# A linear-attention and ELU feed-forward kernel: the second tile cut to two blocks, W_out loaded earlier, and two blocks of second-layer work kept as filler

## The chip, the cores and the metric

The kernel runs on one core of a Trainium2 chip. The metric is the device time of one execution in microseconds (us), the median of several runs. One execution is also taken by the hardware profiler; its trace gives the start and end of every instruction.

The engines have short names in the profile: PE is TensorE's matmuls (PEld its weight loads), DVE is VectorE, ACT is ScalarE, POOL is GpSimd, SP is the engine that issues DMAs for outputs and transposes. A name with a q (SPq, POOLq) is that engine's instruction queue.

## The reference

Decayed linear attention over q, k, v of shape 4 x 8 x 768 x 64 (batch, heads, tokens, head size), then a two-layer feed-forward network with ELU on the 3072 tokens. All inputs and the output are float32.

```python
# attention, per batch and head, blocks of 64 tokens
intra = ((qb @ kb.T) * Dmask) @ vb          # Dmask[i, j] = lam ** (i - j) for i >= j, else 0
inter = (qb * lam_pow) @ kv_state           # lam_pow[i] = lam ** (i + 1)
out[block] = intra + inter
kv_state = lam ** 64 * kv_state + (kb * rev_pow).T @ vb

# feed-forward
x = out.transpose(0, 2, 1, 3).reshape(3072, 512)
h = x @ w_in                                # 512 -> 2048
g = where(h > 0, h, exp(min(h, 0)) - 1)
y = g @ w_out                               # 2048 -> 512
```

## The kernel before

**Blocks.** The kernel takes 128 tokens at a time. A block g (0 to 23) is one such chunk of one batch: g = 4 * chunk + batch, six chunks of four batches. In the change's title and in the prediction "chunk" is used for such a block: blocks 4 and 5 are the second chunk of tokens of batches 0 and 1. From g = 4 on the attention works on pairs (g, g + 1).

**Tiles.** The feed-forward network works on tiles of blocks. `TS` (L37) lists their sizes; `T0` gives each tile's first block and `where` maps a block to its tile and place. Before, there are six tiles of four blocks, 512 tokens each. The first layer of tile t has 16 slices of 128 of the 2048 hidden columns. Slice n takes four matmuls of up to 512 columns into a PSUM bank (`mm1_mm`, L424), then an exp and a relu on ScalarE (L450, L454) and one product on VectorE (L467) that gives g. Its buffers e and r have three copies each, so ScalarE can be at most three slices ahead of VectorE. For slices 2, 4 and 6 of tile 0 VectorE does the relu's part too (L462, L465). `mm1` has a branch for tiles of 256 tokens (`MT == 256`) that no tile takes before: it puts slices n and n + 1 side by side in one bank, and does exp, relu and product on both at once.

**Second layer.** `mm2(t, i, n)` (L499) adds the part of slice n to block i of tile t; after n = 15 the block is copied out of PSUM, by ScalarE for even i (L515) and VectorE for odd i (L513), and stored by SP (L516). The very last block is done by `mm2_last` (L479) in three pieces of 256, 128 and 128 columns.

**Attention of a pair g**, called a visit (`visit`): transposes of q and k on TensorE (`att_T`, L218) with copies by ScalarE (`att_Te`, L230), or for later pairs a DMA transpose on SP (`att_xT`, L274); scaled keys kd on VectorE (`att_kd`, L286); scores (`att_S`, L299); the decay mask on VectorE (`att_mask`, L311); outputs (`att_O`, L325 and L333); the state's update (`att_U`, L371); the outputs scaled into xt, the input of the first layer (`att_X`, L354); the new state on VectorE (`att_st`, L407); and the product of the old state with the decay for the next chunk on POOL (`att_tmp`, L388).

**Order.** Each engine executes in the order in which the program emits instructions. That order is written out by hand. `steps` is a list of (name, first-layer slice, second-layer parts). Steps ('A', 0..15) carry tile 0's first layer; ('B', 0..15) carry second-layer work alone; (1, 0) to (5, 15) carry tiles 1 to 5; ('E', 0) is the rest of the second layer. In each step the first layer's matmuls, exp and relu come first, then what was registered for the step with `at` (visits, loads, transposes), then the ELU product, then the second-layer matmuls:

```python
for s, m1, m2 in steps:
    ...
    er = mm1(t, n, alt=t == 0 and n in (2, 4, 6))
    do(s)
    if er:
        elu(t, n, *er)
    for t2, i2, n2 in m2:
        mm2(t2, i2, n2, "H" if t2 == 0 and m1 is None and i2 > 1 else "M")
```

**Loads.** All inputs are loaded and cast to float16 by DMAs that POOL issues, in the order of `LOADS`. An entry (g, 2) is three DMAs, q, k and v of a pair (L72); ('wi', i) is a piece of W_in (L97); ('wo', i) a quarter of W_out, four slices (L104); ('kd', g) is a product on POOL. The list is cut into stretches that are emitted at given steps, so POOL's products `tmp` stand between them. `XT` says at which step the DMA transposes of a pair are emitted on SP; SP also issues the stores, and waits for each in order.

**Before, around the change.** The second layer of blocks 0 and 1 begins at step ('A', 10); 36 more of its 64 matmuls with those of block 2 fill the B steps, beside the visits of pairs 4 and 6, on which tile 1 depends. Block 3 gives one matmul to each step of tile 1. From tile 2 on each step has four of the tile before. W_out's first two quarters are emitted before the steps, the third and fourth at ('A', 9) and ('A', 10), after the loads of pair 6.

Of the kernel before, what the change touches and what calls it, by code (L numbers as in the profile page):

```python
# [15 lines left out]
def kernel(  # L16
# [10 lines left out]
    nc = tc.nc  # L27

    B, H, S, D = q.shape
# [7 lines left out]
    TS = [4, 4, 4, 4, 4, 4]  # L37
    T0 = [sum(TS[:t]) for t in range(len(TS))]
    NT = len(TS)
    where = {T0[t] + i: (t, i) for t in range(NT) for i in range(TS[t])}  # L40

# [16 lines left out]
    kn = [cpool.tile([128, 2 * H, 64], FP16, name=f"kn_{i}") for i in range(NB)]  # L58
    vn = [cpool.tile([128, 2 * H, 64], FP16, name=f"vn_{i}") for i in range(NB)]

    def emit_load(g, n=1, which="qkv"):
        c, b = divmod(g, B)
        rows = slice(c * L, (c + 1) * L)
        i, o = (g // 2) % NB, (g % 2) * H
        for w, src in (("q", q), ("k", k), ("v", v)):
            if w not in which:
                continue
            if w == "v":
                dst = vn[i][:, o : o + n * H, :]
            else:  # L70
                dst = (qn if w == "q" else kn)[i][:, o : o + n * H, :]
            nc.gpsimd.dma_start(  # L72
                out=dst, in_=src[b : b + n, :, rows].rearrange("b h p d -> p (b h) d")
            )

    def heads(ts, g, n=1):
        o = (g % 2) * H
        return ts[(g // 2) % NB][:, o : o + n * H, :]
# [16 lines left out]
    def emit_wi(i):  # L95
        f0 = sum(WI[:i]) * 128
        nc.gpsimd.dma_start(  # L97
            out=wi_t[i][:],
            in_=moe_w_in[:, f0 : f0 + WI[i] * 128].rearrange("(k p) f -> p k f", p=128),
        )  # L100

    def emit_wo(i):
        f0 = sum(WO[:i]) * 128
        nc.gpsimd.dma_start(  # L104
            out=wo_t[i][:],
            in_=moe_w_out[f0 : f0 + WO[i] * 128, :].rearrange("(n p) f -> p n f", p=128),
        )
# [5 lines left out]
    LOADS = [(0, 1, 'q'), (0, 1, 'k'), (0, 1, 'v'), (1, 1, 'q'), (1, 1, 'k'), (1, 1, 'v'), (2, 1, 'q'), (2, 1, 'k'), (3, 1, 'q'), (3, 1, 'k'), (2, 1, 'v'), (3, 1, 'v'), ('wi', 0), ('wi', 1), ('wi', 2), ('wi', 3), ('wi', 4), ('wi', 5), ('kd', 0), ('wi', 6), ('kd', 2), ('wo', 0), (4, 2), ('wo', 1), (6, 2), ('wo', 2), ('wo', 3), (8, 2), (10, 2), (12, 2), (14, 2), (16, 2), (18, 2), (20, 2), (22, 2)]  # L113

    def run_loads(items):
        for it in items:
            if it[0] == "wi":
                emit_wi(it[1])
            elif it[0] == "wo":
                emit_wo(it[1])  # L120
            elif it[0] == "kd":
                att_kd(it[1], 2, "p")
            else:
                emit_load(*it)
# [53 lines left out]
    ks = cpool.tile([128, H], FP32, name="ks")  # L178
# [101 lines left out]
    def att_kd(g, n, eng="v"):  # L280
        if g // B == NC - 1:
            return
        kd = asb.tile([128, n * H, 64], FP16, tag="kd", name=f"kd{g}", bufs=2)
        ks_b = ks[:].unsqueeze(1).unsqueeze(3).broadcast_to([128, n, H, 64])
        e = nc.vector if eng == "v" else nc.gpsimd
        e.tensor_tensor(  # L286
            out=kd[:].rearrange("p (n h) d -> p n h d", n=n),
            in0=heads(kn, g, n).rearrange("p (n h) d -> p n h d", n=n),
            in1=ks_b, op=ALU.mult,
        )  # L290
        for i in range(n):
            kds[g + i] = kd[:, i * H : (i + 1) * H, :]
# [48 lines left out]
    def att_X(g, n, parts=1):  # L341
        t, i = where[g]
        if i == 0:
            xt[t] = asb.tile([128, HP, TS[t] * L], FP16, tag="xt", name=f"xt{t}")
        po = pS.pop(("O", g))
# [69 lines left out]
    def mm1_mm(t, n, lo, hi, tag="H"):  # L415

        if n == 0 and lo == 0:
            gt[t] = msb.tile([128, NF, TS[t] * L], FP16, tag="g", bufs=2, name=f"g{t}")
        if lo == 0:
            pH_of[t, n] = ps.tile([128, TS[t] * L], FP32, tag=tag, bufs=2, name=f"psH{t}_{n}")  # L420
        pH = pH_of[t, n]
# [49 lines left out]
    def mm2_last(t, i):  # L471

        c, b = divmod(T0[t] + i, B)
        t0 = b * S + c * L
        x0 = 0
        for x, (w, tag) in enumerate([(256, 'M'), (128, 'M'), (128, 'H')]):
            pm = ps.tile([128, w], FP32, tag=tag, bufs=2, name=f"psM{t}_{i}_{x}")
            for n in range(NF):
                nc.tensor.matmul(  # L479
                    pm[:], lhsT=gt[t][:, n, i * L : (i + 1) * L],  # L480
                    rhs=wo_t[wo_at[n][0]][:, wo_at[n][1], x0 : x0 + w],
                    start=(n == 0), stop=(n == NF - 1),
                )
            o = msb.tile([128, w], FP32, tag="osb", bufs=3, name=f"osl{x}")
            (nc.scalar.copy if x % 2 else nc.vector.tensor_copy)(o[:], pm[:])
            (nc.scalar if x % 2 else nc.sync).dma_start(
                out=out[t0 : t0 + L, x0 : x0 + w], in_=o[:]
            )
            x0 += w

    def mm2(t, i, n, tag="M"):
        if T0[t] + i == NG - 1:
            if n == NF - 1:
                mm2_last(t, i)
            return
        if n == 0:
            psM[t, i] = ps.tile([128, DM], FP32, tag=tag, bufs=2, name=f"psM{t}_{i}")
        pm = psM[t, i]
        nc.tensor.matmul(  # L499
            pm[:], lhsT=gt[t][:, n, i * L : (i + 1) * L],  # L500
            rhs=wo_t[wo_at[n][0]][:, wo_at[n][1], :], start=(n == 0), stop=(n == NF - 1),
        )
        if n < NF - 1:
            return
        c, b = divmod(T0[t] + i, B)
        t0 = b * S + c * L
        o = msb.tile([128, DM], FP32, tag="osb", bufs=3, name=f"osb{t}_{i}")
        last = T0[t] + i == NG - 1
        if last:
            raise AssertionError  # L510
        else:
            if i % 2:
                nc.vector.tensor_copy(o[:], pm[:])  # L513
            else:
                nc.scalar.copy(o[:], pm[:])  # L515
            nc.sync.dma_start(out=out[t0 : t0 + L, :], in_=o[:])  # L516
        psM.pop((t, i))
# [16 lines left out]
    def at(s, f, *a, **k):  # L534
        run.setdefault(s, []).append(lambda: f(*a, **k))
# [63 lines left out]

    run_loads(LOADS[17:25])  # L600
    for s, g in zip([], (0, 2)):
        at(s, att_kd, g, 2)
# [6 lines left out]
    XT = {10: (1, 2), 12: (1, 10), 14: (2, 2), 16: (2, 10), 18: (3, 2), 20: (3, 10), 22: (4, 2)}  # L609

    def visit(g, s0, s1, s2):
        if g in XT:
            at(XT[g], att_xT, g)
        else:
            at(s0, att_T, g, 2, "q")
            at(s0, att_T, g, 2, "k")
            at(s0, att_Te, g, 2, "q", "a")
            at(s0, att_Te, g, 2, "k", "v" if g in () else "a")
        if g not in ():
            at(s0, att_kd, g, 2, "p" if g in () else "v")  # L620
        at(s1, att_S, g)
        at(s1, att_S, g + 1)
        at(s1, att_mask, g)
        at(s1, att_mask, g + 1)
        if g in ():
            at(s1, att_kd, g, 2, "p" if g in () else "v")
        at(s2, att_O, g, 2)
        at(s2, att_U, g)
        at(s2, att_X, g, 2)
        at(s2, att_st, g)  # L630
        at(s2, att_tmp, g + B)

# [47 lines left out]
```

## Time and profile before

| | us |
|---|---|
| median of 5 runs (216.96 to 217.62) | 217.19 |
| the profiled execution's own time | 217.09 |
| its span, first to last instruction | 215.3 |
| TensorE busy (95% of the span) | 204.2 |
| VectorE busy (70%) | 151.4 |
| ScalarE busy (59%) | 127.5 |
| POOL busy (37%) | 80.1 |

The page gives busy time per engine, and the span in 40 slices of 5.4 us, each with a digit for the busy share in tenths. PEclk is the granted TensorE clock in the same tenths; the mean was 0.998. A matmul's length in the trace includes the tail of its pipeline, so the next one starts before it ends: the time that TensorE needs is read from start to start. An instruction that waited shows in square brackets the idle time before it and what released it. A DMA's row gives the time from its issue to its landing.

### The profile page before, as it was taken

What the parts mean: (1) busy time and instruction counts of PE and PEld (TensorE: products, weight loads), DVE (VectorE), ACT (ScalarE), POOL (GpSimd) and SP (SyncE); (2) the same over time, 40 slices, a digit from 0 to 9 for tenths busy, and PEclk for the clock granted to TensorE, in tenths of its full rate; (3) what the DMA queues carried; (4) which work ended last, traced back from release to release, by engine and by line L of the source; (5) the groups of instructions that cost most, each with busy time, mean ns of one, the idle gap of its engine ahead of it and who ended that gap; (6) DMA issues with size and microseconds to landing.
All of it is one profiled execution on the core that took longest, in us unless ns stands there. A gap on an engine that the chain in (4) does not pass through costs nothing.

```text
span 215.3 us, 4003 instructions
## 1 busy us (share of the span) xinstructions
PE 204.2 (95%) x1602; PEld 101.4 (47%) x1602; DVE 151.4 (70%) x194; ACT 127.5 (59%) x241; POOL 80.1 (37%) x76
## 2 busy tenths in 40 slices
PE   4888989989999999999999999999999999999992
PEld 1454435545454544545445445445445444444462
DVE  6665999968899999897985785775565544534011
ACT  6757898332978776566466466456556666675110
POOL 8999999995923948580400000000000000000000
PEclk9999999999999999999999999999999999999999
DMA  5999999999999999999961061061011011110222
GB/s 38 148 153 181 206 169 181 177 184 158 209 153 156 155 157 175 172 168 184 163 145 57 0 146 52 0 148 52 0 49 52 0 49 49 50 49 3 97 80 67
DMA packets 98899, 23.86 MB, mean 111 GB/s; under 512 B 90944, under 2 KB 95936, under 8 KB 98880
## 3 DMA queue, kind: packets, MB, share of 16 engines
q0 software_dynamic: 80208, 13.63, 82.9%
q1 hardware_dynamic: 18528, 9.90, 20.3%
q8 instruction: 12, 0.20, 0.4%
q10 hardware_dynamic: 144, 0.07, 0.1%
q14 instruction: 7, 0.06, 0.1%
HBM read 27.27 MB, written 6.29 MB: 156 GB/s over the span
## 4 chain that ended last, share of the span: by engine, by line
PE 79%; DMA 7%; DVE 4%; POOL 4%; ACT 3%; issue 1%; POOLq 0%; DVEq 0%
PE psM L499 35%; PE psH L424 32%; DMA wo<-in_moe_w_out_dram 5%; PE psS L299 3%; PE psO L325 3%; POOL tmp L388 3%; DMA kn<-in_k_dram 2%; PE psO L333 2%; PE psM L479 2%; DVE g L467 1%; PE psW L525 1%; DVE m L462 1%; PE psU L371 1%; ACT qT L230 1%; ACT e L450 1%
## 5 line engine op out<-in xcount | busy, mean ns | idle before, releaser
L424 PE MATMUL psH<-xt,wi 128*128 128x512 f16 (+2 forms) x388 | 97.4, 377 | 0.4 <-ACT r L454 0.3
L467 DVE SCALAR_TENSOR_TENSOR g<-e,r 128x512 f16<-128x512 f32 x93 | 72.1, 797 | 33.9 <-ACT r L454 33.7
L499 PE MATMUL psM<-wo,g 128*128 128x512 f16 x368 | 94.5, 380 | 1.4 <-DMA wo<-in_moe_w_out_dram 0.7
L450 ACT ACTIVATE e<-psH 128x512 f32<-128x512 f32 x96 | 57.5, 599 | 55.1 <-PE psH L424 52.5
L424 PEld LDWEIGHTS <-wi 128*128 128x128 f16 x388 | 37.5, 98 | 45.1 <-issue 1.8
L454 ACT ACTIVATE r<-psH 128x512 f16<-128x512 f32 x93 | 55.3, 595 | 0.0
L499 PEld LDWEIGHTS <-g 128*128 128x128 f16 x368 | 34.5, 98 | 42.0 <-DMA wo<-in_moe_w_out_dram 1.2
L311 DVE TENSOR_TENSOR P<-psS,mask 128x1024 f16<-128x1024 f32 (+1 forms) x28 | 28.7, 1065 | 5.3 <-PE psS L299 5.3
L388 POOL TENSOR_TENSOR tmp<-st,up_p 64x512 f32<-64x512 f16 x16 | 22.6, 1414 | 8.9 <-DVE st L407 7.9
L72 POOL DMA_DIRECT2D vn<-in_v_dram x14 | 15.2, 1093 | 7.3 <-issue 7.3
L72 POOL DMA_DIRECT2D kn<-in_k_dram x14 | 15.2, 1088 | 7.2 <-issue 7.2
L72 POOL DMA_DIRECT2D qn<-in_q_dram x14 | 15.7, 1118 | 2.7 <-issue 2.7
L515 ACT COPY osb<-psM 128x512 f32<-128x512 f32 x12 | 7.0, 591 | 15.9 <-PE psM L499 15.9
L354 DVE TENSOR_TENSOR xt<-psO,qs 128x1024 f16<-128x1024 f32 x10 | 12.2, 1220 | 5.6 <-PE psO L333 5.6
L325 PE MATMUL psO<-P,vn 128*64 128x128 f16 x184 | 11.9, 226 | 0.0
L325 PEld LDWEIGHTS <-vn 128*64 128x64 f16 x184 | 9.6, 112 | 4.7 <-issue 4.0
L513 DVE COPY osb<-psM 128x512 f32<-128x512 f32 x11 | 7.6, 689 | 5.5 <-PE psM L499 5.4
L407 DVE TENSOR_TENSOR st<-tmp,psU 64x512 f16<-64x512 f32 x16 | 10.9, 680 | 0.2
L333 PE MATMUL psO<-qT,st 128*64 128x128 f16 x160 | 10.2, 219 | 0.0
L286 DVE TENSOR_TENSOR kd<-kn,ks 128x1024 f16<-128x1024 f16 x8 | 10.0, 1246 | 0.1
L333 PEld LDWEIGHTS <-st 128*64 128x64 f16 x160 | 9.0, 110 | 0.0
L299 PEld LDWEIGHTS <-kT 64*128 64x128 f16 x192 | 5.6, 97 | 6.5 <-issue 3.0
(60 smaller groups left out, 95.3 us busy)
## 6 DMA issues: line engine op xcount, KB each, us to landing
out_dram<-osb SPq DMA_DIRECT2D x23, 256.0 KB, 2.0
qn<-in_q_dram POOLq DMA_DIRECT2D x10, 256.0 KB, 15.7
kn<-in_k_dram POOLq DMA_DIRECT2D x10, 256.0 KB, 16.1
vn<-in_v_dram POOLq DMA_DIRECT2D x10, 256.0 KB, 16.7
wo<-in_moe_w_out_dram POOLq DMA_DIRECT2D x4, 512.0 KB, 10.8
wi<-in_moe_w_in_dram POOLq DMA_DIRECT2D x2, 512.0 KB, 9.3
wi<-in_moe_w_in_dram POOLq DMA_DIRECT2D x3, 256.0 KB, 7.0
qn<-in_q_dram POOLq DMA_DIRECT2D x4, 128.0 KB, 5.0
```

The lines of the kernel that those rows point to most:

```text
L72: nc.gpsimd.dma_start(out=dst, in_=src[b : b + n, :, rows].rearrange("b h p d -> p (b h) d"))
L299: nc.tensor.matmul(s[:, hh, hp, :], lhsT=kT[g][r, hp, :], rhs=qT[g][r, hp, :], start=True, stop=True,)
L311: nc.vector.tensor_tensor(out=P[:, :, c], in0=s[:, :, c], in1=(mask if g < B else mask1)[:, :, c], op=ALU.mult,)
L325: nc.tensor.matmul(po[r, i, hp, :], lhsT=v_of(g + i, 2 * hp + hh), rhs=P[:, hh, hp, :], start=True, stop=(c == 0), skip_group_check=True,)
L333: nc.tensor.matmul(po[r, i, hp, :], lhsT=st[(g + i) % B // 2][c % 2][:, (g + i) % 2, hp, r], rhs=qT[g + i][:, hp, :], start=False, stop=Tr ...
L354: nc.vector.tensor_tensor(out=dst, in0=po[:, :, c], in1=qs[:, c].unsqueeze(1).broadcast_to([128, n, w, 128]), op=ALU.mult,)
L388: e.tensor_tensor(out=tmp[r], in0=old[r, :, :, r], in1=up_p[r].unsqueeze(1).unsqueeze(3).broadcast_to([64, 2, HP, 64]), op=ALU.mult,)
L424: nc.tensor.matmul(pH[:, lo:hi], lhsT=wi[:, kk, j * 128 : (j + 1) * 128], rhs=xt[t][:, kk, lo:hi], start=(kk == 0), stop=(kk == HP - 1),)
L450: nc.scalar.activation(e[:], pH[:], AF.Exp)
L454: nc.scalar.activation(r[:], pH[:], AF.Relu)
L467: nc.vector.scalar_tensor_tensor(out=g, in0=e[:], scalar=-1.0, in1=r[:], op0=ALU.add, op1=ALU.min)
L499: nc.tensor.matmul(pm[:], lhsT=gt[t][:, n, i * L : (i + 1) * L], rhs=wo_t[wo_at[n][0]][:, wo_at[n][1], :], start=(n == 0), stop=(n == NF - 1),
```

## The change

The tiles become seven: four blocks, then two (blocks 4 and 5), then four times four, and two at the end (22 and 23). The two small tiles take the branch for 256 tokens in `mm1`: eight steps each, with two slices in a bank. The B steps fall from sixteen to five; they finish blocks 0 and 1. Blocks 2 and 3 are held back: four matmuls of them go into each of tile 1's eight steps. Tile 2's sixteen steps get two each of tile 1's two blocks, tiles 3 to 5 four each as before, tile 6's eight steps eight each of tile 5. What is left for 'E' is two blocks instead of four.

Visits move with the tiles: the pairs 6 and 8 into tile 1, 10 and 12 into tile 2, and so on; 22 is alone in tile 5. In `LOADS` the third and fourth quarter of W_out come ahead of pair 6, and all that up to pair 6 is emitted before the steps. The loads of pairs 8 to 22 move to steps from (1, 0) on, and the DMA transposes are emitted at other steps. The last block is done in two pieces, 384 and 128 columns. `att_kd` gets a branch for ScalarE that no step chooses.

```diff
-    TS = [4, 4, 4, 4, 4, 4]
+    TS = [4, 2, 4, 4, 4, 4, 2]
...
     LOADS: 
-    ..., ('wo', 0), (4, 2), ('wo', 1), (6, 2), ('wo', 2), ('wo', 3), (8, 2), ...
+    ..., ('wo', 0), (4, 2), ('wo', 1), ('wo', 2), ('wo', 3), (6, 2), (8, 2), ...
...
-        for x, (w, tag) in enumerate([(256, 'M'), (128, 'M'), (128, 'H')]):
+        for x, (w, tag) in enumerate([(384, 'M'), (128, 'H')]):
...
-    run_loads(LOADS[17:25])
+    run_loads(LOADS[17:27])
...
-    XT = {10: (1, 2), 12: (1, 10), 14: (2, 2), 16: (2, 10), 18: (3, 2), 20: (3, 10), 22: (4, 2)}
+    XT = {10: (1, 12), 12: (2, 4), 14: (2, 12), 16: (3, 4), 18: (3, 12), 20: (4, 4), 22: (4, 12)}
...
     visits, (pair, (transposes and kd, scores and mask, the rest)):
-    (4, (('A', 12), ('A', 14), ('B', 2))), (6, (('B', 7), ('B', 10), ('B', 13))), (8, ((1, 0), (1, 2), (1, 5))),
-    (10, ((1, 8), (1, 10), (1, 13))), (12, ((2, 0), (2, 2), (2, 5))), ..., (22, ((4, 8), (4, 10), (4, 13)))
+    (4, (('A', 12), ('A', 14), ('B', 1))), (6, ((1, 0), (1, 4), (1, 6))), (8, ((1, 8), (1, 12), (1, 14))),
+    (10, ((2, 0), (2, 2), (2, 5))), (12, ((2, 8), (2, 10), (2, 13))), ..., (22, ((5, 0), (5, 2), (5, 5)))
...
     loads at steps, (step, from, to in LOADS):
-    (('A', 9), 25, 26), (('A', 10), 26, 27), (('A', 14), 27, 28), (('A', 15), 28, 29), (('B', 11), 29, 30),
-    (('B', 13), 30, 31), ((1, 1), 31, 32), ((1, 5), 32, 33), ((1, 9), 33, 34), ((1, 13), 34, 35)
+    ((1, 0), 27, 28), ((1, 4), 28, 29), ((1, 8), 29, 30), ((1, 12), 30, 31),
+    ((2, 0), 31, 32), ((2, 3), 32, 33), ((2, 6), 33, 34), ((2, 9), 34, 35)
...
     steps:
-    (('B', 0), None, [(0, 2, 0)]), ..., (('B', 6), None, [(0, 2, 6), (0, 0, 6), (0, 1, 6)]), ..., (('B', 15), ...)
-    ((1, 0), (1, 0), [(0, 3, 0)]), ((1, 1), (1, 1), [(0, 3, 1)]), ...
-    ((2, 0), (2, 0), [(1, 0, 0), (1, 0, 1), (1, 0, 2), (1, 0, 3)]), ...
+    (('B', 0), None, [(0, 0, 6), (0, 1, 6), (0, 0, 7), (0, 1, 7)]), ..., (('B', 4), ...)
+    ((1, 0), (1, 0), [(0, 2, 0), (0, 3, 0), (0, 2, 1), (0, 3, 1)]), ((1, 2), (1, 2), ...), ..., ((1, 14), ...)
+    ((2, 0), (2, 0), [(1, 0, 0), (1, 0, 1)]), ((2, 1), (2, 1), [(1, 0, 2), (1, 0, 3)]), ...
...
+    ((6, 0), (6, 0), [(5, 0, 0), ..., (5, 0, 7)]), ((6, 2), (6, 2), [(5, 0, 8), ..., (5, 0, 15)]), ...
```

The branch of `mm1` that the small tiles take stands in the kernel before already:

```python
pH = ps.tile([128, 2 * MT], FP32, tag="H", bufs=2, name=f"psH{t}_{n}")
for x in range(2):
    wi, j = wi_t[wi_at[n + x][0]], wi_at[n + x][1]
    for kk in range(HP):
        nc.tensor.matmul(pH[:, x * MT : (x + 1) * MT], lhsT=wi[:, kk, j * 128 : (j + 1) * 128],
                         rhs=xt[t][:, kk, :], start=(kk == 0), stop=(kk == HP - 1))
```

## The prediction, made before the changed kernel was run

> **What bounds the kernel now.** I read the page's busy rows and slices first, then TensorE's timeline from 39 us on, then busy time by window, then the rows of POOL and of single DMAs. Busy shares and slices:
>
> ```profile
> PE 204.2 (95%) x1602; PEld 101.4 (47%) x1602; DVE 151.4 (70%) x194; ACT 127.5 (59%) x241; POOL 80.1 (37%) x76
> PE   4888989989999999999999999999999999999992
> DMA  5999999999999999999961061061011011110222
> ```
>
> TensorE bounds: from the ninth slice (43 us) nearly all nines. The DMA engines are full until about 110 us, so the order of the loads decides when each lands. The change leaves TensorE's sum of work alone, so it can only gain where TensorE stands still. TensorE's timeline (start, length, instructions, idle before):
>
> ```profile
> 43.80 0.81 PE L499 MATMUL psM<-wo,g 128*128 128x512 f16 x3
> 45.29 1.45 PE L499 MATMUL psM<-wo,g 128*128 128x512 f16 x6 [0.68 <-DMA wo<-in_moe_w_out_dram]
> ...
> 66.65 1.02 PE L424 MATMUL psH<-xt,wi 128*128 128x512 f16 x4
> 67.65 0.62 PE L299 MATMUL psS<-qT,kT 64*128 64x128 f16 x16
> 68.20 0.39 PE L499 MATMUL psM<-wo,g 128*128 128x512 f16 x1
> ```
>
> The first pair is the stall on the third W_out piece. The second hides a wait: four matmuls take 0.863 us start to start, so scores(10) should have begun 0.1 later than 67.51; they waited for a transpose. Busy time by window (columns: window, length, then busy us by engine, with instruction counts):
>
> ```profile
> 39.02:57.51 18.49, 17.77 (x214) 10.06 (x213) 14.80 (x17) 8.03 (x13) 15.52 (x14) 1.00 2.14 172
> 57.51:76.13 18.62, 18.62 (x181) 9.34 (x181) 18.50 (x23) 14.74 (x28) 10.27 (x9) 1.00 1.82 169
> 76.13:107.90 31.77, 31.77 (x258) 15.60 (x257) 29.62 (x34) 18.39 (x35) 16.49 (x13) 1.00 1.98 169
> ```
>
> Busy is not dense, so I count starts. Dense prices, from stretches without a wait: a 512-wide matmul 0.2158 (76 us on); 16 transposes of a pair 0.90 (53.36 to 54.26); a pair's scores 0.647; its outputs and state update 1.367 (84.56 to 86.79, less 0.863). From 39.02 to 57.51 stand 53 matmuls, two transposes, two scores, two outputs: 11.44 + 1.79 + 1.29 + 2.73 = 17.26, so 1.23 us of 18.49 is idle (0.84 of it start to start at W_out). From 57.51 to 76.13: 69 matmuls, one scores, two outputs = 18.27, so 0.35 is idle. After 76.13 it is dense to 211.5. **All that can be won is 1.58 us.** Everything before 39.02 is the same instructions on TensorE: step A is untouched, and the load of chunk 5's k that it waits for (33.9) keeps its place.
>
> **The change part by part.** (tile, slice) names a step, B a step without first-layer work.
>
> *W_out ahead of chunks 6, 7.* Time to landing of single DMAs gives wo1 at 37.7, q/k/v of 6,7 at 39.5, 41.4, 42.7, wo2 at 45.2, wo3 at 47.8, back to back. Reordered on one queue: wo2 40.2, wo3 42.8, then q6 44.6, k6 46.5, v6 47.8.
>
> *B shortened.* After 39.02: 6 matmuls to 40.3, outputs of 4 to 41.7, 16 matmuls to 45.1. wo2 is wanted at 41.7 and wo3 at 43.4: both there. The 0.84 is gone, and so are the small gaps of 39 to 58.
>
> *Tile 1 of two chunks.* Eight steps of 8 narrow and 4 wide matmuls (1.74 us). ScalarE's exp and relu keep 512 columns at 0.48 us each (start to start, 19.34 to 20.78), and VectorE's product stays at 128x512: their work does not change. (1,0) starts at 45.1; xt is done at about 42.8. Transposes of 6: q at 46.0, k at 46.5, just when k6 lands. That is late next: I take **0.2** (bounds 0 and 1.5, if the queue runs like its slower stretches). Scores 6 at 50.6, outputs 53.0; transposes of 8 at 56.1, outputs of 8 at 62.8, matmuls done at 65.0. (2,0) needs xt of chunk 9: VectorE starts it 0.27 after the last output matmul (50.14 to 50.41) and takes 1.22, so 65.2: **0.2** of wait (0 to 0.8 if VectorE lags; nothing precludes a lag).
>
> *256-wide matmuls.* 128 replace 64. The nearest row is the last block, 16 of 256 and 7 of 128 columns:
>
> ```profile
> 207.82 2.30 PE L479 MATMUL psM<-wo,g 128*128 128x256 f16 x23
> ```
>
> Less 0.22 for the last one's own length and 6 x 0.056 (8 transposes take 0.45), a 256-wide one costs 0.109; two cost 0.002 more than one of 512, times 64: **0.1** (0 to 0.3). Against this speaks the Trainium skill, "TensorE: Matmul & The Clock Gate", "Why this matters for your kernels": with fewer than 512 rows of tokens, pad or keep K contiguous, or the clock oscillates to half. At half clock those matmuls would cost 27.7 instead of 13.9 us, and the sum would be +13. The rows here say 1.00 clock, through 0.84 us of idle and 128-wide matmuls; the trace decides, and I price it at nothing.
>
> *Last block as 384+128.* 16 matmuls fewer at the same 0.002: **-0.04**. The end moves from VectorE with SP's queue (0.29 + 1.6) to ScalarE with its own (0.27 + 1.7): nothing. Tile 6's shorter end saves nothing: TensorE was dense there anyway.
>
> *Loads past POOL's products.* POOL executes in order. Before, chunks 8 to 11 were issued ahead of the product for pair 8; now they stand behind it, and 12, 13 behind that of pair 10:
>
> ```profile
> 36.84 1.18 POOL L72 DMA_DIRECT2D qn<-in_q_dram  x1
> 44.39 3.03 POOL L388 TENSOR_TENSOR tmp<-st,up_p 64x512 f32<-64x512 f16 x2
> 47.37 1.20 POOL L72 DMA_DIRECT2D qn<-in_q_dram  x1
> ```
>
> The product waits for VectorE's state, about 44.2, so q8 is issued near 47.3, not 36.8, while the queue empties at 47.8. How long the restart takes no row shows directly. The nearest: the first load (128 KB) landed 3.7 us after its issue. The Trainium skill, "DMA: Bandwidth & Descriptors", "Anatomy of one DMA - SWDGE (gpsimd) path", gives about 2.0 us plus bytes by 436 GB/s: 2.6 us for 256 KB. By the rule q8 lands near 49.9, as before (49.7): no hole, nothing to pay. By the row, with 0.9 for the second 128 KB at the backlog's 1.8 per 256 KB, it lands at 51.9: a hole of 2.2. I take 1.2, between. Transposes of 8 (56.1) have the room either way. What follows is the transpose of 10 by DMA:
>
> ```profile
> kT<-kn SPq DMA_TRANSPOSE x1, 10.4
> ...
> kT<-kn SPq DMA_TRANSPOSE x1, 3.2
> ```
>
> 10.4 was beside loads (issued at 57.16, when k10 landed), 3.2 without any (110.66). Before, it landed at 67.6 and scores waited. Now: 67.6 + 1.2 = 68.8 against scores(10) at 68.7. I take **0.2** (0 to 1.9). SP's queue: later transposes stand behind output stores. That of 12 follows the store of chunk 3, near 68, and lands by 79.9 against 81.2; that of 16 follows a store at 98.2, lands by 110.2 against about 110. Covered, with under 1.5 us left; without that cover each costs what it is late.
>
> *VectorE in tile 2.* Steps have 2 fillers: 16 x 1.295 + 2 x 2.03 = 24.8 us for 16 products and two visits. VectorE needs 24.1 for that without POOL (12.03 in each of two eight-step windows after 107.9). POOL's products stretch it: three g took 3.57 beside one (83.61) and 1.90 otherwise, so 1.5 per pair, two pairs: 27. A lead of three e buffers (1.9) hides most. Mask(13) is late next: about **0.3** (0 to 1.5).
>
> *Others.* The ScalarE branch of att_kd is never chosen: nothing. Two held-back blocks use M banks freed by copies at 45.8, wanted at 47: nothing. The earlier W_out issues push POOL's first four products by 1.6 us; VectorE's slowdown moves with them, and their reader is at 42.8: nothing.
>
> Sum: -1.58 + 0.2 + 0.2 + 0.1 - 0.04 + 0.2 + 0.3 = -0.62. The profiled execution took 217.09 (span 215.3 and 1.8 around it), so 216.5; the median is 0.1 higher: **216.6**.
>
> **The rivals.**
>
> *The load queue runs dry (slower).* If the product really leaves a hole of its full 3.0 us, k10 lands at 60.1, its transpose at 70.6, scores(10) wait 1.9 instead of 0.2: -0.62 + 1.7 = +1.1, 218.3. It decides once the hole passes 2.3 us (k10 after 59.4): then the gain turns to +0.4. For it: transposes already gated before, and POOL is strictly in order. Against: the hole frees DMA engines, and a transpose alone takes a third. Chance 0.28.
>
> *VectorE becomes the bound of tile 2 (no change).* If the 27 us are not hidden, about 1 us comes back there: 217.2. For it: VectorE was busy 18.50 of 18.62 us in the old tile 1, and 29.62 of 31.77 after. Against: that old tile lost only 0.35. Chance 0.22.
>
> *Nothing new stands in the way.* All new waits zero: 217.19 - 1.58 + 0.06 = 215.7. Chance 0.12; with my sum's own case at 0.38 that makes 0.50 faster.
>
> *The pairing is not done* would be a rival, but mm1 already branches on a tile of 256 columns.
>
> **How the numbers follow.** Faster by over 0.2% (0.43 us, about what a measurement of this kernel can tell from no change): 0.50; within: 0.22; slower: 0.28. Range: from 215.8, all waits nearly gone, to 218.0, most of the dry queue's case. The likeliest case alone: 216.2 to 216.9.
>
> **What would show it.** Right: no W_out wait near 42 to 45; (1,0) at 45 to 46; first 512-wide first-layer matmul of tile 2 near 65; dense from 70; TensorE's end near 210.6 in the span. Wrong: a gap over 1 us at the transposes of 6, at scores(10), or waits of ScalarE's e on VectorE's g in tile 2; k10's transpose issued after 59.4; 256-wide matmuls over 0.115 us apart.

## The result, and the profile after

The changed kernel takes 216.63 us (median of 25 runs) against 217.32 us for the kernel before, run beside it: a ratio of 0.9951, with a 95% interval of 0.9938 to 0.9964. The forecast was 216.6 us. The number was right. The profile shows that the reason was not. Three of the changed kernel's executions (219.2 to 219.4 us, granted clock 0.992) and the profiled one of an experiment below (e5, clock 0.763) were slow ones, and all ratios here compare fast executions alone: those of the changed kernel have a median of 216.4 us.

The page of the kernel after, busy time by engine and the same slices as before:

```profile
span 214.5 us, 4091 instructions
PE 203.6 (95%) x1650; PEld 106.2 (50%) x1650; DVE 151.1 (70%) x193; ACT 128.0 (60%) x241; POOL 77.7 (36%) x76
PE   4888989899999999999999999999999999999994
DMA  6999999999999999999993313214211011111112
```

The profiled execution took 216.24 us, 0.85 less than the one before, and the span is 0.8 shorter. TensorE still bounds; its slices are the same nines. So when does it end? Start, length, instructions and idle time before, in the last microseconds of the kernel before:

```profile
211.61 0.29 DVE L485 COPY osl<-psM 128x128 f32<-128x128 f32 x1 [1.36 <-PE psM L479]
211.92 0.33 SPq L486 DMA_DIRECT2D out_dram<-osl  x1
```

and of the kernel after:

```profile
207.92 3.66 PE L485 MATMUL psM<-wo,g 128*128 128x384 f16 x32
210.72 0.56 DVE L491 COPY osl<-psM 128x384 f32<-128x384 f32 x1 [5.36 <-PE psM L485]
211.30 0.33 SPq L492 DMA_DIRECT2D out_dram<-osl  x1
211.61 0.27 ACT L491 COPY osl<-psM 128x128 f32<-128x128 f32 x1 [2.91 <-PE psM L485]
211.91 0.37 ACTq L492 DMA_DIRECT2D out_dram<-osl  x1
```

The last copy out of PSUM starts at 211.61 in both. TensorE has gained nothing in these two executions. The last store is issued at 211.9 in both and lands 1.6 us later, at 213.5, in both. Yet one program ends at 215.3 and the other at 214.5. **The gain lies behind the last store**, in a part of the program that the prediction priced at nothing.

What became of the 1.58 us that TensorE stood idle before? The third quarter of W_out no longer makes it wait. But it waits elsewhere. TensorE's timeline after:

```profile
39.00 1.46 PE L505 MATMUL psM<-wo,g 128*128 128x512 f16 x6
40.39 0.25 PE L331 MATMUL psO<-P,vn 128*64 128x128 f16 x2
...
41.49 0.25 PE L331 MATMUL psO<-P,vn 128*64 128x128 f16 x2 [0.47 <-DVE P L317]
...
42.31 3.63 PE L505 MATMUL psM<-wo,g 128*128 128x512 f16 x16
45.78 1.04 PE L445 MATMUL psH<-xt,wi 128*128 128x256 f16 x8
46.65 0.61 PE L218 MATMUL psT<-ident,qn 128*128 128x128 f16 x8
47.10 0.61 PE L218 MATMUL psT<-ident,kn 128*128 128x128 f16 x8
...
53.51 0.25 PE L331 MATMUL psO<-P,vn 128*64 128x128 f16 x2
...
54.78 1.04 PE L505 MATMUL psM<-wo,g 128*128 128x512 f16 x4
...
64.66 1.04 PE L505 MATMUL psM<-wo,g 128*128 128x512 f16 x4
65.80 1.04 PE L430 MATMUL psH<-xt,wi 128*128 128x512 f16 x4
...
68.40 1.03 PE L430 MATMUL psH<-xt,wi 128*128 128x512 f16 x4
69.64 0.62 PE L305 MATMUL psS<-qT,kT 64*128 64x128 f16 x16 [0.21 <-DMA kT<-kn]
...
110.17 1.03 PE L430 MATMUL psH<-xt,wi 128*128 128x512 f16 x4
111.39 0.62 PE L305 MATMUL psS<-qT,kT 64*128 64x128 f16 x16 [0.20 <-DMA kT<-kn]
```

Start to start against the dense price of the same piece: the outputs and update of 4 and 5 take 1.92 us (40.39 to 42.31) where the next pair takes 1.27 (53.51 to 54.78): 0.65 lost, to the mask of block 5. Four matmuls before tile 2 take 1.14 instead of 0.86: 0.28, to xt, which VectorE finishes at 65.74. Scores(10) follow their slice after 1.24 instead of 0.96: 0.28. Scores(16) lose 0.26 in the same way (110.17 to 111.39). The narrow matmuls take 0.87 for eight instead of 0.863, 16 times: about 0.1. Together about 1.6 us: all that was won in the middle was spent in the middle.

### The profile page after: what moved, and what is told of

It is laid out like the page before. It is cut to its first block, busy times and chain, and to the rows that moved or that the text cites. A ratio compares the mean times of both kernels' runs of the same rounds, so it can differ in the third digit from the quotient of the medians.

```text
span 214.5 us, 4091 instructions
## 1 busy us (share of the span) xinstructions
PE 203.6 (95%) x1650; PEld 106.2 (50%) x1650; DVE 151.1 (70%) x193; ACT 128.0 (60%) x241; POOL 77.7 (36%) x76
## 4 chain that ended last, share of the span: by engine, by line
PE 58%; POOL 17%; DMA 14%; issue 5%; DVE 4%; ACT 0%; POOLq 0%; DVEq 0%
PE psM L505 29%; PE psH L430 15%; PE psH L445 7%; DMA qn<-in_q_dram 5%; DMA kT<-kn 5%; DMA wo<-in_moe_w_out_dram 4%; POOL qn L72 3%; POOL kn L72 3%; POOL vn L72 3%; POOL wi L97 2%; POOL tmp L394 2%; DVE g L473 2%; PE psO L331 2%; POOL kd L292 2%; PE psM L485 2%
## 5 line engine op out<-in xcount | busy, mean ns | idle before, releaser
L473 DVE SCALAR_TENSOR_TENSOR g<-e,r 128x512 f16<-128x512 f32 x93 | 68.9, 756 | 41.0 <-ACT r L460 40.7
L456 ACT ACTIVATE e<-psH 128x512 f32<-128x512 f32 x96 | 57.5, 599 | 63.1 <-PE psH L430 46.8
L430 PE MATMUL psH<-xt,wi 128*128 128x512 f16 (+2 forms) x324 | 81.2, 376 | 1.0 <-DMA wi<-in_moe_w_in_dram 0.3
L430 PEld LDWEIGHTS <-wi 128*128 128x128 f16 x324 | 31.2, 98 | 38.7 <-issue 1.0
L394 POOL TENSOR_TENSOR tmp<-st,up_p 64x512 f32<-64x512 f16 x16 | 20.2, 1262 | 14.1 <-DVE st L413 13.3
L445 PE MATMUL psH<-xt,wi 128*128 128x256 f16 x128 | 16.6, 273 | 0.0
L445 PEld LDWEIGHTS <-wi 128*128 128x128 f16 x128 | 12.5, 98 | 4.9
L292 DVE TENSOR_TENSOR kd<-kn,ks 128x1024 f16<-128x1024 f16 x8 | 12.4, 1548 | 0.0
```

Source lines behind the costliest of these rows:

```text
L292: e.tensor_tensor(out=kd[:].rearrange("p (n h) d -> p n h d", n=n), in0=heads(kn, g, n).rearrange("p (n h) d -> p n h d", n=n), in1=ks_b, ...
L394: e.tensor_tensor(out=tmp[r], in0=old[r, :, :, r], in1=up_p[r].unsqueeze(1).unsqueeze(3).broadcast_to([64, 2, HP, 64]), op=ALU.mult,)
L430: nc.tensor.matmul(pH[:, lo:hi], lhsT=wi[:, kk, j * 128 : (j + 1) * 128], rhs=xt[t][:, kk, lo:hi], start=(kk == 0), stop=(kk == HP - 1),)
L445: nc.tensor.matmul(pH[:, x * MT : (x + 1) * MT], lhsT=wi[:, kk, j * 128 : (j + 1) * 128], rhs=xt[t][:, kk, :], start=(kk == 0), stop=(kk = ...
L456: nc.scalar.activation(e[:], pH[:], AF.Exp)
L473: nc.vector.scalar_tensor_tensor(out=g, in0=e[:], scalar=-1.0, in1=r[:], op0=ALU.add, op1=ALU.min)
```

## The experiments

### Is it the middle or the end?

The first two experiments part the change. One takes the kernel before and cuts only the last block in two:

```diff
-        for x, (w, tag) in enumerate([(256, 'M'), (128, 'M'), (128, 'H')]):
+        for x, (w, tag) in enumerate([(384, 'M'), (128, 'H')]):
```

> The kernel before, with only its last block done in two pieces (384 and 128 columns) instead of three. Theory A (the prediction's: the gain comes from TensorE's idle time in the middle, the end is worth 0.04 us): no measurable change, 0 to -0.1 us. Theory B (TensorE gained nothing, because its last matmul ends at 211.5 in both profiles; the gain lies in what follows it, where the span after the last copy's start at 211.61 is 3.7 us before and 2.9 after): -0.6 to -0.8 us, and the last copy again near 211.6.

The other takes the changed kernel and undoes this line alone.

> The changed kernel with the last block in three pieces as before. Theory A: keeps the gain, 0.5 to 0.7 us faster than before. Theory B: loses it, within 0.2 us of before, with 3.6 to 3.8 us from the last copy's start to the span's end.

The first took 216.66 us, ratio to before 0.9966 (0.9953 to 0.998). The second took 217.2, ratio 1.0003 (0.9984 to 1.0022). Theory B holds. The one edited line brings 0.7 us by itself. Seven tiles, W_out's order, the fillers and the visits, all together, bring nothing that can be measured; the second interval leaves room for 0.4 us either way.

### What in the last block's line is worth 0.7 us?

Two theories. SP ends the program, and it matters whether SP issues the last store (theory 1), or there is one store fewer (theory 2). The first kernel is the one before with two pieces and the queues exchanged, the second has three pieces with the last on ScalarE's queue:

```diff
-            (nc.scalar.copy if x % 2 else nc.vector.tensor_copy)(o[:], pm[:])
-            (nc.scalar if x % 2 else nc.sync).dma_start(
+            (nc.scalar.copy if x == 0 else nc.vector.tensor_copy)(o[:], pm[:])
+            (nc.scalar if x == 0 else nc.sync).dma_start(
```

> The kernel before with its last block in two pieces, but the queues exchanged: 384 columns by ScalarE and its queue, the last 128 by VectorE and SP. Theory 1 (the end is longer when SP, which ends the program, issues the last store itself at 211.9 us): the gain of the two pieces is lost, within 0.2 us of before, 3.6 to 3.8 us from the last copy's start to the end. Theory 2 (one store fewer to issue and to wait for): the gain stays, 0.5 to 0.8 us faster than before.

(with three pieces the condition is `x == 2`)

> The kernel before, three pieces as before, but the second piece by VectorE and SP and the last by ScalarE and its queue. Theory 1 (who issues the last store): 0.5 to 0.8 us faster than before, about 2.9 us from the last copy's start to the end. Theory 2 (the number of stores): no measurable change.

Two pieces with the last on SP keep the gain: 216.44 us, 0.9965 (0.9944 to 0.9985). Three pieces with the last on ScalarE's queue have none: 217.46, 1.0007 (0.9988 to 1.0026). Theory 1 falls. But the number of stores need not be the reason either. SP's own records at the end say more. (A semaphore is a counter: a DMA raises it when its data has landed, and an engine can wait for it.) SP's semaphore waits at the program's end (operation, count, durations in ns, first and last start), before, from 212.4 us on:

```profile
L675 SPq EVENT_SEMAPHORE  x8: 28/28/28, 213.5 to 214.4; - x8
L675 SPq DRAIN  x2: 7/7/7, 214.5 to 214.5; - x2
```

after, between 211.5 and 212.6, and then from 212.6 on:

```profile
L681 SPq EVENT_SEMAPHORE  x7: 27/28/28, 211.7 to 212.5; - x7
...
L681 SPq EVENT_SEMAPHORE  x2: 28/28/28, 213.2 to 213.6; - x2
L681 SPq DRAIN  x2: 7/10/13, 213.6 to 213.7; - x2
```

In both programs the last store lands at 213.5. After the change SP has gone through seven of its waits while the store was still on its way, and is through 0.1 us after it landed. Before, it stood at the first of the eight waits in the row until 213.5, and the other seven came after it, until 214.4. The DMAs that SP and ScalarE issue get eight semaphores in turn. With three pieces the last store got the first of the eight that SP waits for; with two pieces, the last. That is a third theory: what counts is the last store's turn. To tell it from the number of stores, the turn was moved and the number at the end kept. The kernel before with two pieces, and one store long before the end cut in halves:

```diff
+            if (t, i) == (1, 0):
+                for z in (0, 256):
+                    nc.sync.dma_start(out=out[t0 : t0 + L, z : z + 256], in_=o[:, z : z + 256])
+            else:
-            nc.sync.dma_start(out=out[t0 : t0 + L, :], in_=o[:])
+                nc.sync.dma_start(out=out[t0 : t0 + L, :], in_=o[:])
```

> The kernel before with the last block in two pieces, and block 4's store, long before the end, issued as two halves, so that one more DMA is issued on the hardware queues. The program gives those DMAs eight semaphores in turn, and at its end SP waits for all of them in one fixed order. Theory 3 (what counts is the last store's place in that turn: before, it has the first in the order, so SP goes on through the other waits for about 1 us after it has landed; in the changed kernel it has the last): now the last store has the first semaphore again, and the two pieces lose their gain, within 0.2 us of before, 3.6 to 3.8 us from the last copy's start to the end. Theory 2 (the number of stores at the end): the gain stays, 0.5 to 0.8 us faster than before.

The same with the condition `T0[t] + i in range(4, 11)`, and three pieces:

> The kernel before with three pieces as before, and the stores of blocks 4 to 10 issued as two halves each, seven DMAs more, so that the last store has the last of the eight semaphores. Theory 3: 0.5 to 0.8 us faster than before with three pieces, 2.8 to 3.0 us from the last copy's start to the end. Theory 2: no gain; slower if the extra stores disturb the transposes.

Two pieces with the turn moved by one: 217.44 us, 0.9994 (0.9974 to 1.0014); the gain is gone. Three pieces with the turn moved by seven: 216.73, 0.996 (0.9941 to 0.998); the gain is there, though seven more stores are issued. Theory 3 holds, theory 2 falls. The last copy and store in both, two pieces first:

```profile
211.85 0.27 ACT L485 COPY osl<-psM 128x128 f32<-128x128 f32 x1 [2.91 <-PE psM L479]
212.15 0.37 ACTq L486 DMA_DIRECT2D out_dram<-osl  x1
...
211.81 0.29 DVE L485 COPY osl<-psM 128x128 f32<-128x128 f32 x1 [1.36 <-PE psM L479]
```

Their spans end at 215.6 and 214.6: from nearly the same start one is 3.7 us from its end, the other 2.8. The table puts the kernels side by side. The turn is the place of the last store's semaphore in the order in which SP waits for the eight.

| kernel | pieces | last store | turn of the last store | last copy to end, us | ratio to before |
|---|---|---|---|---|---|
| before | 3 | SP | first | 3.7 | 1 |
| e2, changed, three pieces | 3 | SP | first | 3.7 | 1.0003 |
| e6, last on ScalarE | 3 | ScalarE | first | 3.7 | 1.0007 |
| e9, turn + 1 | 2 | ScalarE | first | 3.7 | 0.9994 |
| changed | 2 | ScalarE | last | 2.9 | 0.9951 |
| e1, two pieces | 2 | ScalarE | last | 2.8 | 0.9966 |
| e5, last on SP | 2 | SP | last | no fast profile | 0.9965 |
| e10, turn + 7 | 3 | SP | last | 2.8 | 0.9960 |

The rows above do not name the semaphores, but the traces' records of the single instructions do, and they agree with every line of this table. The DMAs of SP and ScalarE carry semaphores 100 and 112 to 118 in turn, and SP waits for them at the end in that order. The last store has 100 in the four kernels with "first" and 118 in the four with "last".

### Where the middle's gain went

Mask 5 came late. Before the change, POOL's four products came first, and after them VectorE's keys, two ELU products and the masks of 4 and 5:

```profile
29.46 5.90 POOL L388 TENSOR_TENSOR tmp<-st,up_p 64x512 f32<-64x512 f16 x4
...
35.83 1.21 DVE L286 TENSOR_TENSOR kd<-kn,ks 128x1024 f16<-128x1024 f16 x1
36.97 1.28 DVE L467 SCALAR_TENSOR_TENSOR g<-e,r 128x512 f16<-128x512 f32 x2
38.17 2.34 DVE L311 TENSOR_TENSOR P<-psS,mask 128x1024 f16<-128x1024 f32 x2
```

VectorE's timeline after:

```profile
32.82 1.48 DVE L473 SCALAR_TENSOR_TENSOR g<-e,r 128x512 f16<-128x512 f32 x1 [0.36 <-ACT r L460]
34.22 2.06 DVE L292 TENSOR_TENSOR kd<-kn,ks 128x1024 f16<-128x1024 f16 x1
36.20 2.97 DVE L473 SCALAR_TENSOR_TENSOR g<-e,r 128x512 f16<-128x512 f32 x2
39.10 2.34 DVE L317 TENSOR_TENSOR P<-psS,mask 128x1024 f16<-128x1024 f32 x2
```

and POOL's after:

```profile
25.29 2.27 POOL L104 DMA_DIRECT2D wo<-in_moe_w_out_dram  x3
27.85 1.16 POOL L72 DMA_DIRECT2D qn<-in_q_dram  x1 [0.30 <-DMA wi<-in_moe_w_in_dram]
30.37 1.14 POOL L72 DMA_DIRECT2D kn<-in_k_dram  x1 [1.37 <-DMA wo<-in_moe_w_out_dram]
32.61 1.14 POOL L72 DMA_DIRECT2D vn<-in_v_dram  x1 [1.10 <-DVE g L473]
33.77 6.30 POOL L394 TENSOR_TENSOR tmp<-st,up_p 64x512 f32<-64x512 f16 x4
```

POOL stood still for 2.8 us while it issued pair 6. The records of its loads say for what: they too get eight semaphores in turn (102 to 109), and each issue waits until the load eight places before it has landed. Those before q and k of 6 landed at 27.57 and 30.09, each 0.3 us ahead of the issue; for v it was 32.01, 0.6 ahead. In none of the traces of this case was a load issued less than 0.28 us after that landing. So POOL's four products ran from 33.8 to 40.1 instead of 29.5 to 35.4. Beside them two ELU products took 2.97 us instead of 1.28, and the keys 2.06 instead of 1.21. If that is the cause, the load of pair 6 belongs behind the products:

```diff
-    run_loads(LOADS[17:27])
+    run_loads(LOADS[17:26])
...
+    (('A', 9), 26, 27) is added to the loads at steps
```

> The changed kernel with the load of pair 6 emitted at step (A, 9), behind POOL's first four products instead of ahead of them. Theory A2: in the changed kernel POOL waited 2.8 us for room while it issued that load, so its products slid from 29.5 to 33.8 us, slowed VectorE's keys and ELU products until 40 us, and mask 5 came 0.5 us late for the outputs of 4 and 5; with the products back at 29.5 that wait is under 0.15 us, the load lands no later (W_out is in the queue until 42.8), and the kernel is 0.4 to 0.7 us faster than the changed one. Rival: the mask is late because the scores or the step are later, not because of the products; then no change.

That POOL waited "for room" was a guess; the records show the semaphores. VectorE's timeline with this edit:

```profile
34.44 1.21 DVE L292 TENSOR_TENSOR kd<-kn,ks 128x1024 f16<-128x1024 f16 x1
35.58 0.68 DVE L473 SCALAR_TENSOR_TENSOR g<-e,r 128x512 f16<-128x512 f32 x1
37.34 0.69 DVE L473 SCALAR_TENSOR_TENSOR g<-e,r 128x512 f16<-128x512 f32 x1 [1.08 <-ACT r L460]
37.95 2.35 DVE L317 TENSOR_TENSOR P<-psS,mask 128x1024 f16<-128x1024 f32 x2
```

and TensorE's:

```profile
38.66 1.46 PE L505 MATMUL psM<-wo,g 128*128 128x512 f16 x6
...
41.31 3.63 PE L505 MATMUL psM<-wo,g 128*128 128x512 f16 x16
```

POOL's products now run from 27.7 to 32.8. Keys and ELU products are back at full speed, VectorE even waits, and TensorE's stretch from the second-layer matmuls of (A, 15) to those after the outputs of 4 and 5 falls from 3.31 us (39.00 to 42.31) to 2.65 (38.66 to 41.31): the 0.65 is back. The kernel takes 215.74 us, 0.9933 (0.9907 to 0.996). Its interval overlaps that of the changed kernel, so the profile carries this verdict, not the times alone.

The second suspect was the load queue. The load of pair 8 waits behind POOL's product for that pair and the queue runs dry: q of 8 landed at 53.2 us, 5.4 after the load before it. Moving the loads of pairs 8 and 10 ahead:

```diff
-    ((1, 0), 27, 28), ((1, 4), 28, 29), ...
+    (('A', 15), 27, 28), (('A', 15), 28, 29), ...
```

> The changed kernel with the loads of pairs 8 and 10 emitted at (A, 15), ahead of POOL's product for pair 8. If the queue's dry stretch (pair 8's q landed at 53.2, 5.4 us after the load before it) makes the transpose of 10 late, q of 8 lands by 50, k of 10 by 57.5, scores(10) no longer wait, and the kernel is 0.2 to 0.4 us faster than the changed one. If the transpose's own length under load sets it, or the wait only moves to (2, 0), no change. POOL may wait for room and push the product of 8, which nothing needs before 65 us.

Scores(10) no longer wait (68.74 to 69.70 is the dense 0.96), but the transposes of k of 6 now do, by 0.3 us, and the last copy starts at 211.61 again. It takes 216.32 us, 0.9953 (0.9939 to 0.9966): no change against the changed kernel. Two of the expectations failed: q of 8 landed at 51.0 and k of 10 at 59.0, not by 50 and 57.5. The dry queue is real, but what it costs was not measured alone; the wait that went with it is 0.28 us. In that run k of 6 landed at 47.4 instead of 46.3, because the third quarter of W_out ahead of it already landed 0.9 us later (41.1 instead of 40.2); why is open.

Two more edits were stacked on the mended kernel, to see whether the smaller waits can be had back: pair 16's DMA transpose ahead of the store that held it up on SP (`16: (3, 4)` becomes `16: (3, 0)` in `XT`), and then two second-layer matmuls moved from step (1, 10) to (1, 14).

> The kernel with pair 6's load behind POOL's products, and the DMA transpose of pair 16 emitted at (3, 0), ahead of the store of tile 2's first block, instead of (3, 4). If scores(16) wait for that transpose because it stands behind the store on SP (issued at 99 to 101, landed at 111.3 in the changed kernel), the transpose is issued by 95 and their wait of 0.1 to 0.3 us is gone: 0.1 to 0.3 us faster than the kernel it is built on. If TensorE is already dense there, no change.

> As the kernel before it in this list, with two of the second layer's matmuls moved from step (1, 10) to (1, 14). If tile 2 starts 0.28 us late because xt of block 9 comes after the fillers of (1, 14) are used up, two more fillers of 0.22 us each hide it: tile 2 starts 0.2 to 0.3 us earlier and the kernel gains as much. Rival: the scores of 8, now 0.43 us earlier, wait for their transposes' copies, or the outputs of 9 for their mask; then no change.

The first removes the wait of scores(16) (109.86 to 110.82) and takes 215.71 us, 0.9928 (0.991 to 0.9946): not to be told from the kernel it is built on. With the second, tile 2 starts without a wait (six matmuls from 63.82, the next at 65.13, which is 6 x 0.216), and 0.2 us of it comes back as a wait of the outputs of 9 for their mask. It takes **215.45 us, 0.9921 (0.99 to 0.9941)**, the fastest kernel here. Against the changed kernel it is 0.003 in the ratio, about 0.65 us, and the two intervals just touch; in the profiles the last copy starts 1.2 us earlier (210.38 against 211.61).

## Why the prediction was right in its number and wrong in its reason

**What bounds, and what can be won.** TensorE bounds, and 1.58 us idle was the right size: the waits are gone, as forecast, and W_out landed when it should (40.2 and 42.7). The old wait of scores(10), which the prediction shows without its size, was 0.04 (66.65 to 67.65 is 1.00, where the dense step is 0.96). One of the prediction's signs failed: TensorE's last matmul was to end near 210.6, and it ends at 211.6 (211.5 before).

**Transposes of 6**, priced 0.2: nothing. k landed at 46.3, and they start at 47.10 without a gap.

**xt before tile 2**, priced 0.2: 0.28. **Narrow matmuls**, 0.1: about 0.1, at a granted clock of 1.00; the half clock that the Trainium skill, as cited in the prediction, gives for few rows did not come, and the four matmuls over K of each slice do follow one another, as it asks. **VectorE in tile 2**, 0.3: nothing. The tile from 65.80 to 90.87 lasts 25.07 us, 0.28 of it scores(10), the rest is the dense sum.

**Scores(10)**, priced 0.2: 0.28, by other numbers. The queue's hole was larger than I took (k of 10 landed at 60.4, 3.3 us later than before, not 1.2). By the prediction that meant slower. But the transpose took 9.2 us, not 10.4, and scores(10) were wanted at 69.4, not 68.7. The point from which the slower rival decides was wrong, because it held both of those fixed. For the restart itself the row was nearer than the skill's 2.0 us plus bytes by bandwidth, 2.6 in all: q of 8 landed 6.7 us after its issue (46.53 to 53.26), and even the row's 4.6 was short.

**"The earlier W_out issues push POOL's first four products by 1.6 us; VectorE's slowdown moves with them ...: nothing."** This step failed. They slid by 4.3 us, since POOL also had to wait for the landing of the load eight places before each of pair 6's, and what matters is not who reads them but who works beside them: the keys and ELU products ahead of mask 5. It cost 0.65.

**Scores(16)**, "covered, with under 1.5 us left": 0.26. By the prediction's own numbers, 110.2 against about 110, it was not covered. The transpose landed at 111.3, and scores(16) could have started at 111.13.

**The end**, priced at nothing: -0.8. I compared copies, queues and landings, and these are the same indeed. I left out what follows the last landing, which was in the span all the time: 3.7 us from the last copy to the end, of which copy and store explain 1.9. That the shorter last block would change the last store's turn was no part of the forecast. So the sum was -1.58 + 0.28 + 0.1 + 0.28 + 0.65 + 0.26 = 0 in the middle, and -0.8 at the end. The forecast of -0.62 was right by luck: two mistakes of like size cancelled. The rival "no change" was right on TensorE, though not by VectorE in tile 2.

## What to carry to other kernels

A forecast that comes out right is tested like one that does not: put back each part of the change alone, for two errors may cancel. Where the last copy starts and where the span ends are two numbers, and what lies between them belongs in the sum. In these runs a product on POOL made the keys and ELU products beside it on VectorE longer, so moving a load past it moved that price too. And where loads share semaphores in turn, issuing one earlier can make its engine wait for an older one.

## What the runs showed of the hardware that was not expected

- How long the program takes to end depended on which of eight semaphores in turn the last store had: about 0.9 us from its landing to the end with the last, 1.8 with the first, whatever the number of stores or the issuing queue.
- POOL waited 1.4 and 1.1 us for two issues when pair 6's loads followed three quarters of W_out, at 28 to 33 us, well before the waits of the kernel before (from 41 us on). In every trace a load was issued at least 0.28 us after the landing of the load eight places before it.
- Beside POOL's products two ELU products took 2.97 us instead of 1.28 and the keys 2.06 instead of 1.21; the two masks, which read PSUM and of which the first ran beside them, took 2.34 in both kernels.
- A DMA transpose in the changed kernel took 5.4 to 11.3 us beside loads, and 3.1 to 3.3 once the loads were over.
